# Two routed linear-attention blocks on one core: one load queue, mixed narrow matmuls, scalar_tensor_tensor for small operations, residuals on the TensorE, row-tiled broadcasts

## The chip, the cores and the metric

The kernel runs on one core of one Trainium2 chip. The metric is the device time of one execution in microseconds (us). PE is the TensorE's matmul stream, PEld its weight loads, DVE the VectorE, ACT the ScalarE, POOL the GpSimd, SP the SyncE. "Granted clock" is the TensorE clock that the throttle granted, 1.00 being full speed. In the clock records of before it is 1.00 or 0.50 and nothing else; values between are means over a stretch.

An execution is called slow when it takes over 1.5% more than the fastest of the same kernel in the same set of runs.

## The reference

2048 tokens of 512 channels go through a linear-attention block A and a block B that sends one token through a gated feed-forward, and then through both again with the same weights. "Block one" and "block two" below are the first and the second A+B pair.

```
def A(x, wqkv, wo):                       # 32 heads of 16
    q, k, v = split(x @ wqkv)
    phi = lambda t: where(t > 0, t + 1, exp(t)) + 1e-6
    kv, z = sum over tokens of phi(k) v^T, and of phi(k)      # per head
    o = (phi(q) @ kv) / (phi(q) . z + 1e-6)
    return o @ wo

def B(x, w_r, w_gate, w_up, w_down):
    r = x @ w_r;  i = argmax(r)           # one token of 2048
    y = (silu(x[i] @ w_gate) * (x[i] @ w_up)) @ w_down * sigmoid(r[i])
    return x with y added to row i

x = A_x
x = x + A(layernorm(x));  x = x + B(layernorm(x))
x = x + A(layernorm(x));  x = x + B(layernorm(x))
```

## The kernel before

The kernel is a list of 1120 operations. Each has an engine, the buffers it reads and writes, and one of six general PSUM banks where it needs one; a literal list gives the order and the bank of each buffer. The program is replayed in that order, with semaphores derived from the data. So a change of order or of a bank is a change of that list, and every engine runs its own operations strictly in the listed order.

The parts that the argument touches:

```
# loads: two queues
ldx("sp", 0, 1); ldw("act", "wk", D)            # token tile 0; wk from the ScalarE's queue
ldx("sp", 1, 2); ldw("sp", "wv", 2 * D); ldx("sp", 2, 4) ...

# division by the denominator: the reciprocals (rden, 32 rows per group m) are spread over
# the 128 channels by a matmul with a 0/1 matrix, then multiplied into phi(q)
for m in range(NC_D):                           # NC_D = 4
    bb = bank()
    A("pe",  e.matmul(B(bb), sel[:, m, :], rden[:, j, :]))      # 128 rows, 512 columns
    A("dve", e.tensor_tensor(pqT[:, m, cols], pqT[:, m, cols], B(bb), ALU.mult))

# output tile t of block L
A("pe", four matmuls pqT x Mw into bank ob)
if L == 1 and t in (14, 15):                    # residual by an identity matmul into the bank
    ...
else:                                           # residual on VectorE
    A("dve", e.scalar_tensor_tensor(out=x_tok[:, t, :], in0=x_tok[:, t, :], scalar=scal,
                                    in1=B(ob), op0=mult, op1=add, accum_out=s1[L][:, t:t + 1]))
    A("act", e.activation(junk, x_tok[:, t, :], ACTF.Square, accum_out=s2[L][:, t:t + 1]))

# small statistics on VectorE (128 x 1 to 128 x 16), for instance
e.tensor_scalar(m_, s1[L][:, sl], 1.0 / D, None, op0=mult)
e.tensor_tensor(stat[0][:, 0, sl], rs[1][:, sl], ic[:, sl], mult)

# the final scaling x * us + b of tiles 0 to 10 is on GpSimd, of 11 to 15 on ScalarE
```

The routed feed-forward of the one token is 14 groups of eight matmuls with one column each (L906), and 56 more for the down projection.

Of the kernel before, what the change touches and what calls it, by code (L numbers as in the profile page):

```python
# [24 lines left out]
2 14 26 5 11 12 15 13 10 0 24 34 55 23 6 16 1 21 35 53 25 22 4 17 20 19 46 18 3 52 47 29 33 30 8 31 32 50 9 73  # L25
54 7 57 56 74 58 49 71 59 60 51 72 61 75 83 76 62 48 63 77 80 78 84 85 149 79 96 163 150 86 94 87 81 151 97 88
153 95 164 89 64 90 82 152 167 154 92 91 65 98 174 66 99 165 67 168 100 68 155 93 101 166 175 69 170 70 103
107 102 156 171 27 129 160 108 116 157 104 172 118 181 158 161 173 28 177 182 159 188 140 178 119 141 117 191
105 179 120 189 138 121 195 192 180 162 193 122 36 196 169 176 123 198 194 106 37 125 139 124 109 127 202 142
110 199 111 130 128 38 114 183 143 131 281 126 203 144 39 40 147 132 184 133 41 112 115 223 42 185 145 43 219  # L30
148 224 186 44 45 226 200 187 220 113 134 201 230 227 221 216 146 136 222 190 217 258 228 137 231 229 205 135
197 206 212 207 254 329 213 208 330 251 214 325 255 326 215 209 256 328 327 240 210 204 241 211 218 252 247
242 257 259 243 237 248 282 233 249 238 283 250 277 234 284 225 235 289 236 297 290 278 232 291 309 279 292
261 280 273 310 262 311 285 274 263 312 265 286 275 264 244 287 276 266 288 239 267 245 269 268 246 270 253
260 298 321 271 331 333 332 334 299 305 322 272 335 323 300 306 345 324 336 301 307 346 308 339 302 341 337
340 343 347 317 303 344 338 342 348 304 352 354 318 349 350 313 319 355 293 353 314 351 416 315 294 320 359
417 295 316 418 356 296 360 421 425 423 422 469 361 365 424 470 426 419 471 362 357 420 358 474 476 478 475
368 436 479 433 370 477 371 372 366 430 373 374 363 367 472 427 375 473 364 369 376 522 393 431 392 383 377
483 378 523 386 428 379 432 480 434 381 380 524 437 489 429 394 385 484 435 529 382 525 490 531 395 486 438
526 396 439 599 532 397 491 441 530 595 442 398 443 487 600 527 444 399 606 459 596 481 400 445 528 597 388  # L40
401 602 607 402 446 598 405 447 407 533 448 458 603 410 440 461 408 449 403 384 406 409 482 411 387 601 460
462 534 542 488 452 493 404 535 539 450 543 492 485 389 536 604 540 451 544 456 605 620 541 537 454 569 453
616 571 621 390 494 391 570 546 572 609 495 573 457 496 574 586 585 512 497 513 617 463 623 498 610 618 455
499 630 624 619 611 575 634 500 625 538 576 612 631 626 613 577 501 632 578 584 502 635 464 579 608 587 588
503 412 633 637 614 545 511 505 504 547 615 514 515 548 644 638 580 549 550 562 561 648 506 645 639 551 465
646 640 622 649 627 581 509 552 647 553 554 466 560 413 555 628 507 516 467 641 415 414 510 468 563 564 558
517 629 642 662 556 508 636 663 582 643 651 557 589 672 652 590 559 655 673 653 650 674 654 656 693 583 675
787 694 518 695 565 566 665 568 567 519 683 666 520 521 667 686 684 668 755 687 763 688 756 689 690 757 764
758 657 765 691 799 696 788 766 679 789 676 790 680 591 681 592 677 767 593 594 707 682 708 669 768 711 709
713 727 710 769 715 700 728 712 716 670 714 721 770 729 717 701 722 718 723 800 724 702 719 725 658 801 726  # L50
812 806 810 804 842 805 720 843 802 807 659 775 730 731 808 739 776 732 660 740 733 741 777 661 734 742 735
778 743 736 664 737 703 671 738 809 746 678 811 747 744 685 748 745 749 759 750 751 760 752 753 761 754 762
783 803 814 819 795 813 815 816 784 817 818 785 796 692 820 704 846 821 786 797 771 823 822 798 705 824 779
825 772 826 697 773 780 827 774 828 781 698 782 829 830 831 835 699 836 791 833 837 832 706 838 792 834 839
859 865 793 864 863 866 851 860 794 867 861 852 855 840 868 853 862 925 856 854 871 926 875 857 877 872 869
927 873 858 881 870 878 876 930 874 928 934 882 879 929 847 935 883 969 848 931 890 888 970 891 849 886 884
932 887 971 841 885 844 974 889 972 845 978 975 904 880 973 895 899 903 905 907 896 979 906 900 913 933 897
892 901 898 944 893 902 948 850 908 894 909 914 945 1013 976 910 949 1014 940 977 911 1015 936 941 912 950 980
915 917 937 946 916 1022 918 952 953 942 981 1018 921 1016 988 938 1019 922 1017 1020 982 984 920 924 954 1021
955 956 919 992 1023 985 1024 923 989 986 1028 993 990 961 1037 1025 996 994 1029 1026 1032 960 997 962 1030  # L60
1038 965 1042 1043 998 1027 1040 1039 1044 1031 1033 964 983 987 991 999 995 1045 939 1047 943 1000 1034 947
1001 963 1046 951 1048 1056 1004 1036 1002 1041 1051 1035 957 1003 1005 1058 958 1006 966 1057 1059 967 959
1010 1049 1060 1062 1061 1067 1063 1052 1068 1069 1065 1007 1050 968 1070 1071 1072 1073 1086 1064 1009 1074
1075 1080 1076 1087 1081 1066 1053 1008 1077 1082 1083 1012 1088 1078 1054 1011 1084 1079 1085 1055 1090 1114
1089 1091 1115 1092 1099 1094 1095 1096 1093 1101 1097 1102 1103 1100 1098 1104 1106 1107 1105 1108 1109 1110
1111 1112 1113 1116 1117 1118 1119
"""
BANKS = "303121405672141533202544041250322442535534223501015014433142145253206703250251515044105234030302200131345423544131055442341231215412510530451452232042310010052134345231205420132415041105443453024103350410501554523412023315540231"
# [176 lines left out]
def bass_interleave_layers__linear_attn_block__moe_arch_mod__prompt_kernel(  # L245
# [13 lines left out]
    with ExitStack() as es:  # L259
# [63 lines left out]
        usx = SB("usx", [P, NT], F32)  # L323
        nmr = SB("nmr", [P, NT], F32)
# [90 lines left out]
        ldx("sp", 0, 1)  # L415
        ldw("act", "wk", D)
        A("act", lambda e: e.preload_act_table_set("natural_log_exp_and_others"), writes=["table"], est=1300,
          name="table")
        ldx("sp", 1, 2)
        ldw("sp", "wv", 2 * D)  # L420
        ldx("sp", 2, 4)
# [28 lines left out]
        C("pool", lambda e: e.memset(stat[0][:, 3, :], 1.0), ["stat3"], est=100)  # L450
        C("pool", iota(iota_s[:], [[512, NC_D], [1, P]], -16), ["iota_s"], est=600, name="ios")
        DMA("pool", wr_col[:], B_w_r.rearrange("(c p) -> p c", p=P), ["wr_col"], 4096, "ldwr", after=[ldx3])
        DMA("pool", wr_bc[:], B_w_r.rearrange("(o d) -> o d", o=1).to_broadcast([P, D]), ["wr_bc"], TB, "ldwrb",
# [55 lines left out]

        kv_ctr = [0, 0]  # L510
# [6 lines left out]
        BT = (14, 15)  # L517
# [42 lines left out]
        def kv_out(L, kba, kbb):  # L560
# [35 lines left out]
            if L == 1:  # L596
                rb = bank()

                def rmm(e):
                    ins = None  # L600
                    for m in range(NC_D):
                        ins = e.matmul(B(rb)[:, 2 * m:2 * m + 2], kvT[:, m, :], wow_hl[:, m, :], start=True,
                                       stop=True)
                    return ins
                A("pe", rmm, reads=["kvT", "wow_h", "wow_l"], writes=[rb], est=116, name="mr")
                A("dve", lambda e: e.tensor_reduce(mr_f[:], B(rb)[:, 0:8].rearrange("p (m k) -> p m k", k=2), AX.X,
                                                   ALU.add), reads=[rb], writes=["mr_f"], est=170, name="mrf")
                A("dve", lambda e: e.tensor_copy(mr_hl[:, :, 0], mr_f[:]), reads=["mr_f"], writes=["mr_h"], est=155,
                  name="mrh")
                A("dve", lambda e: e.tensor_tensor(mr_hl[:, :, 1], mr_f[:], mr_hl[:, :, 0], ALU.subtract),  # L610
                  reads=["mr_f", "mr_h"], writes=["mr_l"], est=155, name="mrl")
# [20 lines left out]

        def small(fn, reads, writes, name, est=155, eng="dve"):
            return A(eng, fn, reads=reads, writes=writes, est=est, name=name)
# [19 lines left out]
        def xn_tile(t, mean_ap, scale, nbias, reads, eng, tag):  # L654
# [4 lines left out]
            else:  # L659
                A("pool", lambda e: e.tensor_scalar(xn_tok[:, t, :], x_tok[:, t, :], scale[:, t:t + 1],  # L660
                                                    nbias[:, t:t + 1], op0=ALU.mult, op1=ALU.add),
                  reads=[f"x{t}"] + reads, writes=[f"xn{t}"], est=840, name=f"{tag}xn{t}")
# [26 lines left out]
        dctr = [0]  # L689

        def den_group(L, tg):
# [5 lines left out]
            def den(e):  # L697
# [5 lines left out]
            A("pe", den, reads=[f"pq{tg}_{m}" for m in range(NC_D)] + ["Za", "Zb"], writes=[db], est=500,  # L703
# [4 lines left out]
              reads=[f"lden{j}"], writes=[f"rden{j}"], est=629, name=f"A{L}rden{tg}")  # L708
            for m in range(NC_D):
                bb = bank()  # L710
# [479 lines left out]
        for tg in range(4):  # L1190
# [3 lines left out]
            for g in FG:  # L1194
                if g[0] // 4 == tg:
                    final_group(g, ["pool" if t < 11 else "act" for t in g])
# [58 lines left out]
```

## Time and profile before

Three runs gave 179.29 us (179.17 to 180.23). The profiled execution took 180.61 us, spans 178.8 us, and had a mean clock of 0.932.

| what (profile of before) | value |
|---|---|
| PE busy / VectorE busy | 163.9 / 132.8 us |
| first kv projection starts | 9.66 us |
| last output matmul of block one ends | 81.32 us |
| last router matmul of block one | 108.17 us |
| routed feed-forward starts | 114.61 us |
| row projections of the patched token start | 130.54 us |
| last output matmul of block two ends | 162.36 us |
| last matmul of all starts (routed row, block two) | 175.67 us |

From the profile page: busy times, and the span cut into 40 slices of 4.5 us. Each digit is the busy share of a slice in tenths; PEclk is the granted clock in tenths.

```profile
PE 163.9 (92%) x1393; PEld 84.2 (47%) x1393; DVE 132.8 (74%) x415; ACT 112.3 (63%) x293; POOL 77.4 (43%) x127
...
PE   6599997999999999999999999999999989986393
...
DVE  5699999445589999997961368742466999999830
...
PEclk9999999999999999999999999955799999999555
```

PE is nearly full from slice 7 on (counted from 0), VectorE is full in three stretches (about 9 to 31 us, where PE is full too, 54 to 80 us, and 139 to 165 us), and the clock is halved in slices 26 to 28 and in the last three. The chain of waits that ended last says the same:

```profile
PE 63%; DVE 29%; DMA 3%; POOL 1%; issue 1%; ACT 1%; SPq 0%; POOLq 0%
```

The windows view puts numbers on stages. Its columns are the stretch in us, its length, the busy time and number of instructions of PE, PEld, DVE, ACT and POOL in this order, the granted clock, the DMA share and GB/s.

```profile
57.00:73.00 16.00, 15.89 (x81) 6.54 (x81) 16.00 (x43) 12.15 (x35) 3.37 (x5) 1.00 0.04 9
...
113.00:117.00 4.00, 4.00 (x114) 3.29 (x112) 2.84 (x14) 1.20 (x2) 1.29 (x3) 1.00 0.02 4
117.00:121.00 4.00, 4.00 (x51) 2.96 (x47) 1.26 (x4) 0.61 (x3) 0.00 (x0) 0.51 0.01 4
121.00:124.00 3.00, 3.00 (x61) 2.10 (x60) 1.30 (x6) 0.90 (x3) 0.61 (x1) 0.50 0.00 0
...
145.00:162.70 17.70, 16.96 (x103) 7.51 (x104) 17.70 (x55) 11.78 (x38) 4.47 (x6) 1.00 0.08 31
```

In the first and the last of these lines VectorE is busy for the whole stretch. From 113 to 117 us PE runs 114 matmuls, most of them narrow, at full clock; right after it the clock is 0.5. The records give 10.24 us at half clock from 117.1 us on. The timeline of PE and VectorE (start, us, engine, line, operation, shape, count) shows what this costs, and a small operation that stalls:

```profile
64.74 0.81 PE L711 MATMUL ps<-rden,sel 128*128 128x512 bf16 x3
...
67.99 0.38 PE L711 MATMUL ps<-rden,sel 128*128 128x512 bf16 x1
68.20 1.03 PE L728 MATMUL ps<-Mw,pqT 128*128 128x512 bf16 x4
...
78.02 0.16 DVE L808 TENSOR_SCALAR stat<-rs 128x2 f32<-128x2 f32 x1
78.10 0.59 DVE L799 SCALAR_TENSOR_TENSOR nms<-mv,cs 128x4 f32<-128x4 f32 x1
...
119.40 1.87 PE L620 MATMUL ps<-xnT,wqkv 128*128 128x512 bf16 x4
```

The four 512-wide matmuls at 119.40 span 1.87 us, against 1.02 to 1.04 us for four at full clock elsewhere in this trace. The broadcasts are spread: three in a row, or one alone between output matmuls. The operation at 78.10 writes 128x4 elements and takes 0.59 us; its neighbour at 78.02 (128x2) takes 0.16, and so does one of the same size and form at 78.90 (not shown).

### The profile page before, as it was taken

The page shows a single profiled execution, that of the slowest core. Times are in us where ns is not written, and L with a number is a line of the kernel's source. Part 1 is how long each engine was busy: PE and PEld are TensorE (multiplying, and loading weights), DVE is VectorE, ACT ScalarE, POOL GpSimd, SP SyncE. Part 2 cuts the span into 40 slices and gives each one's busy share as a digit, 9 for nine tenths or more (in the row PEclk, how much of TensorE's full clock was granted, in tenths as well). Part 3 has the DMA queues.
Part 4 walks back from the last instruction along what each step waited for, and adds up shares of the span by engine and source line. Part 5 has one row for each costly group of instructions (what it writes and reads, how often), then busy time and mean ns, then how long its engine had stood idle before and what let it go on. Part 6 is the DMA issues. An engine that isn't in the chain of part 4 may idle for free.

```text
span 178.8 us, 3791 instructions
## 1 busy us (share of the span) xinstructions
PE 163.9 (92%) x1393; PEld 84.2 (47%) x1393; DVE 132.8 (74%) x415; ACT 112.3 (63%) x293; POOL 77.4 (43%) x127
## 2 busy tenths in 40 slices
PE   6599997999999999999999999999999989986393
PEld 2244552554454344454555545685544334434382
DVE  5699999445589999997961368742466999999830
ACT  2287754566569569979975467313456936868920
POOL 5049499544654303084899253501225220336500
PEclk9999999999999999999999999955799999999555
DMA  5995425389960000215144200000000000030450
GB/s 144 396 371 115 64 59 105 72 272 369 377 222 0 0 4 0 59 32 113 37 90 91 59 0 0 4 0 4 0 0 5 0 0 0 0 121 5 168 183 4
DMA packets 23257, 15.83 MB, mean 89 GB/s; under 512 B 15656, under 2 KB 21800, under 8 KB 23112
## 3 DMA queue, kind: packets, MB, share of 16 engines
q1 hardware_dynamic: 22632, 14.95, 28.3%
q10 hardware_dynamic: 528, 0.52, 0.9%
q0 software_dynamic: 80, 0.13, 0.6%
q8 instruction: 11, 0.18, 0.4%
q14 instruction: 6, 0.05, 0.1%
HBM read 9.83 MB, written 2.10 MB: 67 GB/s over the span
## 4 chain that ended last, share of the span: by engine, by line
PE 63%; DVE 29%; DMA 3%; POOL 1%; issue 1%; ACT 1%; SPq 0%; POOLq 0%
PE ps L537 27%; PE ps L620 13%; PE ps L728 8%; DVE pqT L713 6%; DVE x_tok L744 5%; PE ps L554 4%; PE ps L906 3%; DMA x_tok<-in_A_x_dram 3%; DVE scr L480 2%; DVE pqT L506 2%; PE ps L932 2%; PE ps L711 1%; DVE st L667 1%; DVE Mw L594 1%; DVE pk L506 1%
## 5 line engine op out<-in xcount | busy, mean ns | idle before, releaser
L504 POOL TENSOR_SCALAR Eb<-Eb 128x512 bf16<-128x512 bf16 x64 | 39.4, 621 | 59.3 <-ACT Eb L502 50.0
L537 PE MATMUL ps<-wqkv,xnT 128*128 128x512 bf16 x256 | 60.3, 380 | 1.4 <-DVE pk L506 1.3
L502 ACT ACTIVATE Eb<-ps 128x512 bf16<-128x512 f32 x64 | 37.5, 596 | 24.8 <-PE ps L620 12.4
L537 PEld LDWEIGHTS ps<-wqkv,xnT 128*128 128x128 bf16 x256 | 23.7, 98 | 27.7 <-DVE pk L506 1.8
L620 PE MATMUL ps<-xnT,wqkv 128*128 128x512 bf16 x128 | 33.6, 402 | 0.1
L506 DVE SCALAR_TENSOR_TENSOR pk<-ps,Eb 128x512 bf16<-128x512 f32 x32 | 21.6, 686 | 14.4 <-POOL Eb L504 12.0
L728 PE MATMUL ps<-Mw,pqT 128*128 128x512 bf16 x128 | 30.4, 379 | 0.8 <-DVE pqT L713 0.6
L506 DVE SCALAR_TENSOR_TENSOR pqT<-ps,Eb 128x512 bf16<-128x512 f32 x32 | 21.4, 686 | 7.7 <-POOL Eb L504 6.6
L544 ACT ACTIVATE va<-ps 128x512 bf16<-128x512 f32 x32 | 18.7, 596 | 9.2 <-PE ps L537 8.9
L750 ACT ACTIVATE junk<-x_tok 128x512 bf16<-128x512 bf16 x30 | 18.6, 621 | 7.8 <-DVE x_tok L744 7.7
L713 DVE TENSOR_TENSOR pqT<-pqT,ps 128x512 bf16<-128x512 bf16 x32 | 20.3, 680 | 0.0
L728 PEld LDWEIGHTS ps<-Mw,pqT 128*128 128x128 bf16 x128 | 11.8, 98 | 15.8 <-DVE pqT L713 2.5
L620 PEld LDWEIGHTS ps<-xnT,wqkv 128*128 128x128 bf16 x128 | 12.1, 101 | 13.6 <-issue 2.4
L660 POOL TENSOR_SCALAR xn_tok<-x_tok,cs,nms 128x512 bf16<-128x512 bf16 x16 | 12.2, 773 | 9.7 <-DVE stat L813 9.1
L1112 POOL TENSOR_SCALAR xn_tok<-x_tok,us,stat 128x512 bf16<-128x512 bf16 x11 | 8.3, 772 | 13.6 <-DVE mv L777 9.0
L554 PE MATMUL ps<-va,pk 128*128 128x129 bf16 x128 | 12.4, 231 | 0.0
L667 DVE BATCH_NORM_STATS2 st<-x_tok 128x6 f32<-128x512 bf16 x16 | 10.4, 674 | 2.2 <-DMA x_tok<-in_A_x_dram 2.2
L554 PEld LDWEIGHTS ps<-va,pk 128*128 128x128 bf16 x128 | 9.6, 104 | 3.8 <-ACT va L544 0.2
L660 POOL TENSOR_SCALAR xn_tok<-x_tok,rs,nms 128x512 bf16<-128x512 bf16 x12 | 10.9, 915 | 0.4 <-DVE mv L669 0.2
L744 DVE SCALAR_TENSOR_TENSOR x_tok<-x_tok,ps 128x512 bf16<-128x512 bf16 x16 | 10.5, 680 | 0.0
L630 ACT ACTIVATE lnv<-mv,eps_col 128x2 f32<-128x2 f32 (+2 forms) x20 | 5.4, 289 | 8.1 <-DVE mv L669 5.6
L744 DVE SCALAR_TENSOR_TENSOR x_tok<-x_tok,stat,ps 128x512 bf16<-128x512 bf16 x14 | 10.0, 735 | 0.0
(204 smaller groups left out, 194.6 us busy)
## 6 DMA issues: line engine op xcount, KB each, us to landing
out_dram<-xn_tok SPq DMA_DIRECT2D x8, 256.0 KB, 2.1
wu<-in_B_w_up_dram SPq DMA_DIRECT2D x2, 896.0 KB, 8.6
wd<-in_B_w_down_dram SPq DMA_DIRECT2D x2, 896.0 KB, 10.5
wg<-in_B_w_gate_dram SPq DMA_DIRECT2D x2, 896.0 KB, 11.8
wqkv<-in_A_wqkv_dram SPq DMA_DIRECT2D x2, 512.0 KB, 8.7
x_tok<-in_A_x_dram SPq DMA_DIRECT2D x1, 1024.0 KB, 8.7
wqkv<-in_A_wqkv_dram ACTq DMA_DIRECT2D x1, 512.0 KB, 5.3
x_tok<-in_A_x_dram SPq DMA_DIRECT2D x1, 512.0 KB
```

The lines of the kernel that those rows point to most:

```text
L502: A("act", lambda e: e.activation(Eb[:, i, :], src(), ACTF.Exp), reads=[b, "table"], writes=[f"E{i}"], est=600, name=name + "E")
L504: A("pool", lambda e: e.tensor_scalar(Eb[:, i, :], Eb[:, i, :], 1.0, 0.0, op0=ALU.min, op1=ALU.max), reads=[f"E{i}"], writes=[f"E{i}"], es ...
L506: return A("dve", lambda e: e.scalar_tensor_tensor(out=dst, in0=src(), scalar=1e-6, in1=Eb[:, i, :], op0=ALU.max, op1=ALU.add), reads=[b, ...
L537: ins = e.matmul(B(b), xT[:, c, t * P:(t + 1) * P], wqkv[:, c, lo:lo + D], start=(c == 0), stop=(c == NC_D - 1))
L544: A("act", lambda e: e.activation(va[:, i, :].rearrange("p (m k) -> p m k", k=129)[:, :, 0:P], B(vb).rearrange("p (m k) -> p m k", k=P), A ...
L554: ins = e.matmul(views[m], pk[:, i, m * P:(m + 1) * P], va[:, i, m * 129:(m + 1) * 129], start=(first and m in (0, 3)), stop=False, skip_g ...
L620: ins = e.matmul(B(qb), wqkv[:, c, qc * P:(qc + 1) * P], xnT[L][:, c, tg * 512:(tg + 1) * 512], start=(c == 0), stop=(c == NC_D - 1))
L660: A("pool", lambda e: e.tensor_scalar(xn_tok[:, t, :], x_tok[:, t, :], scale[:, t:t + 1], nbias[:, t:t + 1], op0=ALU.mult, op1=ALU.add), r ...
L713: A("dve", (lambda e, m=m, bb=bb: e.tensor_tensor(pqT[:, m, cols], pqT[:, m, cols], B(bb), ALU.mult)), reads=[bb, f"pq{tg}_{m}"], writes=[ ...
L728: ins = e.matmul(B(ob), pqT[:, m, t * P:(t + 1) * P], Mw[:, m, :], start=(m == 0), stop=(m == NC_D - 1 and not xb))
L744: A("dve", lambda e: e.scalar_tensor_tensor(out=x_tok[:, t, :], in0=x_tok[:, t, :], scalar=scal, in1=B(ob), op0=ALU.mult, op1=ALU.add, acc ...
L750: A("act", lambda e: e.activation(junk[:, j, :], x_tok[:, t, :], ACTF.Square, accum_out=s2[L][:, t:t + 1]), reads=[f"x{t}", "table"], writ ...
```

## The change

Its intent: take work off the engine that binds in each stage, and keep PE's clock up.

1. Loads on one queue in the order of need: tiles 0 and 1 in one transfer, then tiles 2 and 3, and wk later.
2. The order is rebuilt so that the feed-forward's narrow groups lie between 512-wide groups.
3. Small VectorE operations become scalar_tensor_tensor (STT).
4. In block two the residuals of tiles 3, 7, 11 and 13 go to PE (identity matmul), with GpSimd preparing those tiles in block one and ScalarE evicting; the final scalings are redistributed (GpSimd 6, ScalarE 5, VectorE 5).
5. The broadcasts become one operation of four 32-row matmuls, each with its own 32 of the 128 rows.

The diff, cut to its core. The order and bank lists are replaced as a whole; most small operations change as the ones shown do.

```
-        ldx("sp", 0, 1)
-        ldw("act", "wk", D)
...
-        ldx("sp", 1, 2)
-        ldw("sp", "wv", 2 * D)
+        ldx("sp", 0, 2)
+        ldw("sp", "wk", D)
+        ldx("sp", 2, 4)
+        ldw("sp", "wv", 2 * D)
...
+        def tt(dst, a, c, op, ...):            # was tensor_tensor
+            return stt(dst, a, 1.0, ALU.mult, c, op, ...)
+        def ts_op(dst, a, s, op, ...):         # was tensor_scalar; one() is a broadcast column of ones
+            return stt(dst, a, s, op, one(shape or dst.shape), ALU.mult, ...)
...
-        BT = (14, 15)
+        XBN = (14, 15)
+        XBA = (3, 7, 11, 13)
+        XB = XBA + XBN
...
+            bbs = [bank() for _ in range(NC_D)]
+                def bcast(e):
+                    for m in range(NC_D):
+                        r = slice(32 * m, 32 * m + 32)
+                        ins = e.matmul(B(bbs[m]), sel[r, m, :], rden[r, j, :], start=True, stop=True)
-            for m in range(NC_D):
-                bb = bank()
-                A("pe", (... e.matmul(B(bb), sel[:, m, :], rden[:, j, :], start=True, stop=True)), ...)
...
+            elif xb:                            # tiles 3, 7, 11, 13 of block two
+                A("act", e.activation(x_tok[:, t, :], B(ob), ACTF.Identity, accum_out=s1[L][:, t:t + 1]))
+                A("act", e.activation(junk[:, j, :], B(ob), ACTF.Square, accum_out=s2[L][:, t:t + 1]))
...
+            for t in xx_:                       # the tiles of XB, in block one
+                A("pool", e.tensor_scalar(x_tok[:, t, :], x_tok[:, t, :], usx[:, t:t + 1],
+                                          nmrx[:, t:t + 1], op0=mult, op1=add))          # "Mx2"
...
-                    final_group(g, ["pool" if t < 11 else "act" for t in g])
+                    final_group(g, ["pool" if t < 6 else ("act", "dve")[t % 2] for t in g])
```

## The prediction

> **What bounds the kernel now.** The instruction profile spans 178.8 us. The chain of waits is 63% PE and 29% VectorE. The windows view gives the stages: from 10 to 137 us PE has no idle worth naming (9.5 to 10.0 us busy in nearly every 10); from 137 to 162.7 us VectorE binds (25.4 of 25.7 us busy); from 162.7 us on there is only the latency chain of the last routed row.
>
> **The clock.** Granted clock is 1.00 except from about 117.1 to 127.3 us and from about 165 us: 0.50. The slow stretch of 10.24 us follows the routed feed-forward: eight-matmul narrow groups run back to back from 114.6 us. Inside it a group of four 512-wide matmuls takes 1.73 us instead of 0.86. It holds 12 to 14 such matmuls (2.7 us lost) and about 20 of 129 columns (1 us lost, estimate): about 3.7 us, nearly all on the chain. [...] In the new order no run of narrow matmuls exceeds the four gathers (1.75 us); the 24 feed-forward pieces are split by 512-wide groups. I think the clock stays full there (75%). The end stays at half clock: no wide work is left.
>
> **Row tiling.** 32 broadcasts of 0.216 us become eight sets of four with 32 rows each. The denominator, four column tiles, occupies about 0.35 us a set (151.14 to 151.47 us); by analogy a set falls from 0.86 to about 0.4 us, 3.5 us of PE in all. Half is in block two, where VectorE binds, and is worth nothing there; in block one VectorE is also full (16.0 of 16.0 us from 57 to 73). I count 1 us.
>
> **Residuals on PE.** Four VectorE residuals (0.68+0.08 us each, 3 us) leave the VectorE-bound stage; PE gains 4 x 0.22 us, ScalarE a reading pass of about 0.8 us per tile (18.9 of 25.7 us busy: room), GpSimd 4 x 0.77 us earlier. Against it, VectorE gets five final scalings of 0.4 us, mostly in the tail. Net 2 us.
>
> **Small VectorE ops as scalar_tensor_tensor.** I expect almost nothing from the conversion itself. Stalled small ops (0.45 to 0.60 instead of 0.15 us) occur beside GpSimd's 512-wide work, but scalar_tensor_tensor with two SBUF inputs stalls already: 0.59 us at 78.10, 0.54 at 156.72. [...] The tail loses about 2 us to such stalls, and they shrink because GpSimd keeps 6 instead of 11 final scalings; VectorE's own scalings take back about half. Net 1 us.
>
> **Loads.** Tiles 0 and 1 in one first transfer, wk no longer beside them: tile 0 landed near 6.4 us, should land near 4; first projection 9.66 us, now about 8.7. Net 1 us, as PE is saturated after it.
>
> Sum: 2.8 (expected clock) + 1 + 2 + 1 + 1, less about 0.3 for copies of statistics and GpSimd's added work from 80 to 100 us (already 67 to 86% busy) = 7.5.
>
> **Prediction: 171.8 us, 80% range 168.0 to 176.0. Faster by over 2%: 0.87; within 2%: 0.11; slower: 0.02.**
>
> **What would show it.** Clock row full until the last stage; broadcast sets near 0.4 us; first projection before 9 us; VectorE-bound stage 2 us shorter; scalar_tensor_tensor small ops still showing 0.4 to 0.6 us stalls beside GpSimd.
>
> **What would make it wrong.** A clock drop in the gathers [...]; four banks held per broadcast set delaying PE; GpSimd late with block two's normalised tiles; a gain in PE absorbed by VectorE.

The sum is 2.8 + 1 + 2 + 1 + 1 − 0.3 = 7.5 us, off before's 179.3. The 2.8 us for the clock is three quarters of the 3.7 us estimated from the trace of before; the 75% was my own estimate.

## The result

The kernel after took 174.69 us (median of 4 runs, 174.48 to 174.85) against 179.76 us for before on the same chip (4 runs, 179.17 to 180.37). The ratio of the times is 0.972, with a 95% interval of 0.968 to 0.976: faster by more than 2%. Ratios here and below are the mean time of one kernel's fast runs over that of the other's fast runs of the same rounds, so they are not quite the ratio of the medians I quote. The time of the profiled execution is not in the later sets' ratios.

The profile after spans 172.9 us at a mean clock of 0.971. It is of a run at full clock, while the profile of before is of one of its slowest (0.932), so the two profiles lie 5.9 us apart where the medians lie 5.1. The same lines as before, page first:

```profile
PE 157.7 (91%) x1397; PEld 80.3 (46%) x1397; DVE 131.3 (76%) x420; ACT 113.4 (66%) x301; POOL 74.6 (43%) x125
...
PE   7999999699998988999999999999999799996492
...
DVE  6965999946387999999864456953675899999931
...
PEclk9999999999999999999999999999999999999855
```

PE's busy time fell by 6.2 us, VectorE's by only 1.5. The clock row has no drop before the end stage. In the chain, PE gave way to VectorE:

```profile
PE 47%; DVE 44%; ACT 4%; POOL 2%; issue 2%; POOLq 0%
```

Windows of after:

```profile
57.00:73.00 16.00, 14.54 (x78) 5.74 (x76) 16.00 (x43) 12.24 (x42) 3.55 (x6) 1.00 0.06 12
...
80.00:90.00 10.00, 9.57 (x54) 4.13 (x52) 7.77 (x32) 8.02 (x28) 9.26 (x14) 1.00 0.44 89
...
113.00:117.00 4.00, 4.00 (x68) 2.57 (x65) 1.58 (x3) 1.28 (x3) 1.29 (x3) 1.00 0.00 0
117.00:121.00 4.00, 4.00 (x62) 2.58 (x60) 1.29 (x5) 2.30 (x7) 1.23 (x2) 1.00 0.00 0
```

In the first line VectorE is again busy for 16.00 of 16 us, while PE has dropped from 15.89 to 14.54: the broadcasts are cheaper, but PE now stands idle for 1.46 us. Of that, 1.03 us lies before one set of broadcasts (65.39 us, below); the trace names a ScalarE operation that ended at 65.37 us, and VectorE's multiplication of the set before ended at 65.33, so the wait cannot be put down to one of them. From 80 to 90 us GpSimd is busy for 9.26 us (6.71 in before). The timeline shows the broadcasts and some stalled small operations:

```profile
65.39 0.39 PE L734 MATMUL ps<-rden,sel 32*128 32x512 bf16 x4 [1.03 <-ACT lden L724]
65.72 3.63 PE L758 MATMUL ps<-Mw,pqT 128*128 128x512 bf16 x16
...
79.69 0.77 POOL L678 TENSOR_SCALAR xn_tok<-x_tok,cs,nms 128x512 bf16<-128x512 bf16 x1 [2.23 <-DVE x2w L521]
...
79.80 0.16 DVE L521 SCALAR_TENSOR_TENSOR stat<-rs,ic 128x4 f32<-128x4 f32 x1
79.88 0.59 DVE L521 SCALAR_TENSOR_TENSOR stat<-rs,ones_mat 128x2 f32<-128x2 f32 x1
...
159.45 0.64 DVE L521 SCALAR_TENSOR_TENSOR stat<-stat,nmr 128x4 f32<-128x4 f32 x1
```

Four broadcasts take 0.33 us from the first to the next matmul (65.39 to 65.72), where four full-height ones took 0.86. The stalls are there as before, now in STT. The small operation at 79.88 begins while GpSimd's scaling of 79.69 runs and ends with it, at 80.47; the one at 79.80 began beside the same scaling and was not held. This is the pattern of both traces: of the 42 stalled small operations of before and after (over 0.26 us; counts under e2), 40 end within 0.03 us of the end of the GpSimd operation beside which they began. They are not slow; they wait it out.

Where did the time go, along the kernel? The table gives the moment at which each kernel's PE had issued the same amount of matmul work. It is my own sum over the trace: each matmul at its full-clock time, leaving out the broadcasts, the identity residuals and the warm-up, which differ. The weight given to narrow matmuls matters: another choice moves single rows by up to 0.5 us.

| before, us | after, us | after minus before |
|---|---|---|
| 8.5 | 7.5 | −1.1 |
| 47.0 | 45.7 | −1.3 |
| 68.0 | 67.9 | −0.1 |
| 81.3 | 80.4 | −0.8 |
| 93.4 | 93.6 | +0.2 |
| 111.5 | 111.9 | +0.4 |
| 128.3 | 124.2 | −4.1 |
| 145.3 | 139.6 | −5.6 |
| 159.7 | 154.1 | −5.7 |
| 171.7 | 165.7 | −6.0 |

So at 111 us, two thirds through, the new kernel is no further than the old one. Its head start from the loads is used up in block one. About 4.5 us come in the routed feed-forward, where before ran at half clock, and some 1.9 after it.

### The profile page after: what moved, and what is told of

The parts are those of the page before. It is cut to its first block, busy times and chain, and to the rows that moved or that the text cites. A ratio compares the mean times of both kernels' runs of the same rounds, so it can differ in the third digit from the quotient of the medians.

```text
span 172.9 us, 3813 instructions
## 1 busy us (share of the span) xinstructions
PE 157.7 (91%) x1397; PEld 80.3 (46%) x1397; DVE 131.3 (76%) x420; ACT 113.4 (66%) x301; POOL 74.6 (43%) x125
## 4 chain that ended last, share of the span: by engine, by line
PE 47%; DVE 44%; ACT 4%; POOL 2%; issue 2%; POOLq 0%
PE ps L560 16%; PE ps L641 11%; DVE pqT L743 11%; DVE x_tok L780 8%; DVE pk L506 5%; PE ps L493 4%; PE ps L938 3%; PE ps L577 3%; DVE st L685 3%; DVE pqT L506 3%; DVE scr L480 2%; PE ps L899 2%; PE ps L758 2%; PE ps L964 2%; DVE stat L521 2%
## 5 line engine op out<-in xcount | busy, mean ns | idle before, releaser
L641 PE MATMUL ps<-xnT,wqkv 128*128 128x512 bf16 x128 | 31.0, 379 | 0.8 <-DVE pqT L743 0.8
L678 POOL TENSOR_SCALAR xn_tok<-x_tok,cs,nms 128x512 bf16<-128x512 bf16 x16 | 12.2, 774 | 14.6 <-DVE nms L834 11.9
L786 ACT ACTIVATE junk<-x_tok 128x512 bf16<-128x512 bf16 x26 | 16.2, 622 | 3.2 <-DVE x_tok L780 2.8
L641 PEld LDWEIGHTS ps<-xnT,wqkv 128*128 128x128 bf16 x128 | 11.6, 98 | 12.6 <-DVE pqT L743 1.1
L678 POOL TENSOR_SCALAR xn_tok<-x_tok,rs,nms 128x512 bf16<-128x512 bf16 x12 | 10.2, 857 | 9.8 <-DVE mv L687 7.9
L1131 POOL TENSOR_SCALAR xn_tok<-x_tok,us,stat 128x512 bf16<-128x512 bf16 x6 | 4.7, 796 | 17.7 <-DVE stat L1119 17.7
L577 PE MATMUL ps<-va,pk 128*128 128x129 bf16 x128 | 11.4, 221 | 0.3 <-DVE pk L506 0.3
L577 PEld LDWEIGHTS ps<-va,pk 128*128 128x128 bf16 x128 | 8.9, 98 | 5.9 <-issue 0.9
L493 PE MATMUL ps<-zeros 128*128 128x512 bf16 x18 | 6.4, 537 | 1.2 <-DVE sign L436 1.2
```

The lines of the kernel that those rows point to most:

```text
L577: ins = e.matmul(views[m], pk[:, i, m * P:(m + 1) * P], va[:, i, m * 129:(m + 1) * 129], start=(first and m in (0, 3)), stop=False, skip_g ...
L641: ins = e.matmul(B(qb), wqkv[:, c, qc * P:(qc + 1) * P], xnT[L][:, c, tg * 512:(tg + 1) * 512], start=(c == 0), stop=(c == NC_D - 1))
L678: A("pool", lambda e: e.tensor_scalar(xn_tok[:, t, :], x_tok[:, t, :], scale[:, t:t + 1], nbias[:, t:t + 1], op0=ALU.mult, op1=ALU.add), r ...
L786: A("act", lambda e: e.activation(junk[:, j, :], x_tok[:, t, :], ACTF.Square, accum_out=s2[L][:, t:t + 1]), reads=[f"x{t}", "table"], writ ...
```

## The experiments

All kernels gave correct results. Each ran with its profile and then five rounds (e9 and e11: six) beside the kernel before, in four sets on three chips. The record calls each of these comparisons with before "unclear"; before's own runs spread, as told next. What each part is worth is therefore read from marks. Marks are read from the profiles; within one order they repeat to about 0.02 us once the start (which jitters by up to 0.5 us) is taken off. One run of before at 236 us, far from all others, is left out of every number here.

One warning for reading the ratios. Before's own runs fall into groups by mean clock: in these four sets, 10 of 45 had a clock of 0.967 or more and took 176.4 to 177.3 us; the 33 with less than 0.96 had a median of 179.4 us. In the result's own four runs of before, none was that short. In later sets some were, and only those and runs up to 1.5% longer are "fast". So later ratios are nearer to 1 for the same kernel, and I compare marks, and run times at equal clock.

### The clock and the mixing of narrow matmuls

**c_after**: the kernel after, unchanged, as a control in a later set.

> The changed kernel itself again, as the control of this job and to see whether its own time is one number. Three of six runs of the form with plain small operations showed a mean granted clock of 0.96 instead of 0.97 and 1.6 us more. Theory [...]: two groups of runs about 1.6 us apart, the slower one with the lower mean clock. Rival (the mixed order never falls): one group near 174.7 us, clock 0.96 to 0.972.

Measured: 176.1 us median; three runs at 174.88 to 175.67 us with a clock of 0.965 to 0.971, and three at 176.52 to 176.66, all at 0.959. Ratio 0.990 (0.980 to 1.001). The profiled run was one of the long ones. Its windows show why:

```profile
137.00:145.00 8.00, 6.60 (x32) 2.05 (x29) 6.23 (x12) 4.89 (x10) 0.99 (x2) 0.79 0.00 0
```

A clock of 0.79 over 8 us is 3.4 us at half clock, in a place where before and after had none; the records say 3.41 us. PE is idle for 1.5 us between 130 and 140 us just before it; in the profile after, the same idle time was followed by no drop. From the first output matmul of block one to that of block two every mark is 0.50 to 0.51 us later than in the profile after (the start), and the last output matmul 1.96 us later. So one such stretch cost 1.45 us, and the new kernel meets it in some runs.

**e5_bunched**: the kernel after, with the narrow groups of the feed-forward put together again in one stretch of about 2.8 us; only the order list changes.

```
 order: B0g0 B0u0 ... B0g6 | every remaining B0g*, B0u* moved to here, back to back
```

> The changed kernel with the 14 groups of narrow matmuls of the routed row's first feed-forward products moved into one bunch of 2.8 us; no work is added. Theory (the mixing matters through the granted clock): the clock falls to 0.5 near 115 us for 3.4 to 10.2 us, and the kernel is 2.0 to 4.5 us slower. Rival (the mixing matters through what waits for what): the clock row stays full and the time within 0.7 us.

Measured: 176.52 us (174.98 to 177.10), ratio 0.988 (0.980 to 0.996). In the profile, the clock fell at once:

```profile
113.00:117.00 4.00, 4.00 (x80) 2.58 (x78) 0.87 (x2) 0.38 (x1) 0.66 (x2) 0.71 0.02 4
117.00:121.00 4.00, 4.00 (x25) 2.04 (x23) 0.99 (x3) 1.98 (x7) 0.61 (x1) 0.86 0.00 0
```

Half clock for 3.41 us, and all marks from the down projection on are 1.63 us later; from the first output matmul up to there they are as in after within 0.02. The direction held; the size is short of the 2.0 us expected. It is close to that of one half-clock stretch in c_after, so little is left for the order itself. The trace shows no PE idle time between 110 us and the drop (114.72 us); the last 2.8 us before it are the narrow groups. One of the six runs (174.98 us, clock 0.965) seems to have escaped it.

**e6_before_mixed**: the kernel before, with only its feed-forward order changed (and two buffers' banks exchanged for it): pieces of one or two narrow groups between 512-wide ones.

```
-order: ... B0u0 B0g0 B0u2 B0g2 B0u4 B0g4 B0u6 B0g6 B0u8 B0g8 ... (ten in a row)
+order: ... B0u0 A1q1_1E B0g0 ... A1kv9 A1q0_1 B0u4 B0g4 ... A1kv10 A1q1_3 ... B0u8 B0g8 ...
```

> The kernel before, with only the order around the routed row's feed-forward changed: its narrow groups are cut into four pieces by 512-wide groups that were due later. Theory (the granted clock is what the mixing buys): the clock row is full until the last stage and the span is 3 to 4.5 us below the 178.8 us of the profile of before, which had 10.24 us at half clock; against the mean of the fast runs of before, whose mean clock differs from run to run, 1.5 to 3.5 us. Rival (order alone): within 0.7 us.

Measured: 178.19 us (177.92 to 178.55), ratio 1.004 (0.995 to 1.013). The profile has full clock until the end stage and ends 2.6 us before that of before. But its runs, at clocks of 0.957 to 0.967, take 178.2, and the two runs of before on the same chip that escaped the drop take 176.6. So in the old order mixing removes the halved clock (the profile shows it, and the six runs lie within 0.63 us) and costs about 1.6 us of its own: it makes the time steadier, at 1.1 us under before's median of 179.3, and not faster than before at its best.

**What follows for the clock.** 176.6 us against 174.7 to 174.9 us is before and after both without a drop (before's from other sets than the result's). So of the 5.1 us between the medians of the result, about 1.8 us is work and order, and 3.2 us (179.76 less 176.6) is the clock.

### The broadcasts

**e1_bc_full**: the kernel after, with four full-height broadcasts in place of the 32-row ones, in the same place.

```
-                        ins = e.matmul(B(bbs[m]), sel[r, m, :], rden[r, j, :], start=True, stop=True)
+                        ins = e.matmul(B(bbs[m]), sel[:, m, :], rden[:, j, :], start=True, stop=True)
```

> The changed kernel with the broadcast's four matmuls put back to the full 128 rows (same order, same banks): a set should take 0.86 us of PE again instead of 0.33, 4.3 us of PE over eight sets. Theory (VectorE paces both output stages, so PE time there is not on the chain): 0.3 to 1.2 us slower than the changed kernel. Rival (PE time counts in full, as PE was the engine of most of the chain before): 3.5 to 4.3 us slower.

Measured: 177.43 us (176.90 to 177.91), ratio 0.995 (0.988 to 1.001). The start is 0.35 us late; the last output matmul of block one is 2.02 us late, of block two 3.12, the end 2.76. Row tiling is worth about 2.4 us in the new order: 1.7 gained in block one's output stage (0.4 given back by the routing), 1.1 more in block two. Both expectations missed: it is more than I had allowed, and less than the PE time saved. That saving is itself smaller than 0.86 less 0.33 suggests, because the step from a full-height matmul into a 32-row set takes 0.31 us where it takes 0.22 into a full-height one: from the matmul before a set to the one after it, where nothing waits, it is 0.64 us in after and 1.08 here. (From the first of four to the next full-height matmul, 0.86 against 0.33 us is 2.6 times; with the longer step into the set counted, 0.86 against 0.42 us, 2.0 times.) Over the eight sets, waits included, the sums are 8.19 and 11.75 us, 3.6 us apart. From 57 to 73 us VectorE waits 2.0 us for these broadcasts in e1, and not at all in after.

**e7_before_rowtile**: the kernel before with 32-row broadcasts, nothing else.

```
-            e.matmul(B(bb), sel[:, m, :], rden[:, j, :], start=True, stop=True)
+            e.matmul(B(bb), sel[32 * m:32 * m + 32, m, :], rden[32 * m:32 * m + 32, j, :], start=True, stop=True)
```

> The kernel before with each broadcast matmul reading only the 32 rows it needs, so that neighbours in the queue can overlap; order and banks untouched. In that order the four of a set are often apart. Undone in the changed kernel this part cost 2.75 us. Theory (overlap needs neighbours): gain of 0.5 to 2 us here. Rival (the size alone counts): 2.5 us or more.

Measured: 179.98 us (176.78 to 180.66), ratio 1.006 (0.987 to 1.025); the end mark differs from before's by +0.04 us. Nothing, where the theory had 0.5 to 2. The timeline of PE in e7 shows the reason, at the place quoted from before above:

```profile
64.69 0.44 PE L711 MATMUL ps<-rden,sel 32*128 32x512 bf16 x3
...
68.04 0.39 PE L711 MATMUL ps<-rden,sel 32*128 32x512 bf16 x1
68.36 1.04 PE L729 MATMUL ps<-Mw,pqT 128*128 128x512 bf16 x4
```

In the old order the broadcasts are not four in a row. Five of the 32 stand alone. From a lone 32-row broadcast to the next full-height matmul it is 0.32 us, from a lone full-height one 0.22 us, and the step into it takes 0.31 us against 0.22: each costs 0.2 us more. Only neighbours overlap (0.003 to 0.004 us from one to the next): at the three places where three stand in a row and nothing waits, the stretch from the matmul before to the one after falls to 0.63 us from 0.86 to 0.96. In the other sets later members start 0.06 to 0.6 us apart. Over all 32, waits included, these stretches sum to 11.34 us in before and 11.57 in e7, so PE saved nothing. The gain of row tiling comes from tiling and reordering together; neither the tiling in the old order nor, as e1 shows, the new order without the tiling has it.

### Residuals and small operations

**e3_res_dve**: the kernel after with the residuals of tiles 3, 7, 11, 13 back on VectorE (and GpSimd's and ScalarE's work for them gone).

```
-        XBA = (3, 7, 11, 13)
+        XBA = ()
```

> The changed kernel with the residuals of tiles 3, 7, 11 and 13 of block two back on VectorE; GpSimd's four scalings for them and eight small copies of statistics are gone too. Theory: the stage that VectorE bounds (about 137 to 157 us) gets up to 3 us longer, the stretch from 77 to 93 us, where GpSimd works 86 to 93% of the time, up to 1 us shorter; in sum 1.0 to 2.5 us slower than the changed kernel. Rival (what VectorE saves is eaten by the added scalings): within 0.5 us.

Measured: 175.98 us (175.87 to 179.65, one slow), ratio 0.988 (0.980 to 0.997). Marks against after: the same to the last output matmul of block one; from the last router matmul of block one (102 us) to the first output matmul of block two 0.93 us earlier; the last output matmul 0.26 us later; the end 1.31 us later. So moving these residuals saves 2.2 us at the end and costs 0.93 us in block one: net 1.3. Of the 2.2 us, 1.2 come up to the last output matmul and 1.06 between it and the gather (5.07 us in after, 6.13 here, 6.15 in before): VectorE's last residual ends at 158.10 us here, 0.36 us after the last output matmul, and at 156.39 in after, 1.09 us before it.

**e10_mx2_late**: the kernel after, with that preparation moved. GpSimd's six scalings "Mx2" start at 86.8 to 97.2 us in after, between the normalisations that the transposed tiles of block two wait for; here they start at 100.1 to 115.3 us. Eight copies of statistics on VectorE move too. Order only.

> The changed kernel with GpSimd's six scalings for the residuals on PE, and eight small copies of statistics on VectorE, moved from the stretch of 77 to 93 us, where GpSimd is busy 86 to 93% of the time, to the stretch from 95 to 115 us, where it is half idle. Theory (this is what the residuals on PE cost, 0.93 us at 100 us in the run that took them off): 0.6 to 1.2 us faster than the changed kernel at equal clock. Rival (the loss is only moved): within 0.3 us.

Measured: 174.43 us (173.81 to 175.05), ratio 0.983 (0.973 to 0.993), on the chip where c_after had 176.1. Against c_after, whose profile starts 0.1 us later, the last router matmul comes 1.06 us sooner and the row projections 0.70. At equal clock (0.971) the runs are 174.22 against 174.88 us, one run each. This fits e3: the 0.93 us are mostly the place of this preparation, and 0.6 to 0.7 us of them can be had back by order alone.

**e2_plain_small**: the kernel after, with all converted small operations as tensor_tensor and tensor_scalar again.

```
-            return stt(dst, a, 1.0, ALU.mult, c, op, reads, writes, name, est)
+            return small(lambda e: e.tensor_tensor(dst, f(a), f(c), op), reads, writes, name, est)
-            return stt(dst, a, s, op, one(shape or dst.shape), ALU.mult, ...)
+            return small(lambda e: e.tensor_scalar(dst, f(a), s, None, op0=op), ...)
```

> The changed kernel with its two helpers for small VectorE operations issuing tensor_tensor and tensor_scalar again instead of scalar_tensor_tensor, nothing else. Theory [...]: within 0.5 us of the changed kernel, and 0.4 to 0.6 us stalls of small operations in like number (17 in the changed kernel's trace). Rival (the form matters): 1.5 us or more slower, with clearly more stalls.

Measured: 175.92 us (174.44 to 176.48), ratio 0.986 (0.977 to 0.994); three runs with a clock of 0.967 to 0.971 at 174.44 to 175.37, and three at 176.5 with 0.959 to 0.960, like c_after's run with a drop. All marks are 0.10 to 0.21 us later, and the first projection is 0.21 us late already. The conversion by itself is worth nothing that can be seen. The count of stalls agrees: of the small operations (STT, tensor_tensor, tensor_scalar, cast; up to 64 elements a partition) that began beside a 512-element GpSimd operation, 20 of 60 took over 0.26 us in after and 19 of 60 in e2 (22 of 67 in before). Of the 108 that began with none running, none did in after. Two inputs are not a condition: five of the 22 in before (two casts and three tensor_scalar, one of them 0.60 us at 165.81) read a single tensor.

### The loads

**e4_two_queues**: the kernel after, with wk on the ScalarE's queue from the start and tiles 0 and 1 as two transfers.

```
-        ldx("sp", 0, 2)
-        ldw("sp", "wk", D)
+        ldx("sp", 0, 1)
+        ldw("act", "wk", D)
+        ldx("sp", 1, 2)
```

> The kernel after with the start of its loads undone: wk from a second queue (ScalarE) at the start, token tiles 0 and 1 as two transfers of 128 KB. Theory (the load gain of about 1 us is real and stays): the first transposes come 0.7 to 1.2 us later, and the end of the profile too, 0.7 to 1.3 us later than after's 172.9. Rival (the gain is given back in block one's output stage, where VectorE paces both kernels): the start is late by as much, but the difference is under 0.4 us from the last output matmul of block one on, and the end moves by under 0.4 us.

Measured: 176.1 us (175.94 to 177.45), ratio 0.994 (0.988 to 1.000). The first transposes are 1.34 us later than in after, and so is everything else, to the end: +1.46 at block one's output stage, +1.40 at the last matmul. Tiles 0 and 1 landed at 3.69 us in after; here tile 0 landed at 3.54 and tile 1 at 5.59 (before: 4.36 and 6.43). The theory held: a microsecond at the start is a microsecond at the end. The head start that the table of equal work shows vanishing in block one was not absorbed by a stage that VectorE paces; it was spent on other things there. The 0.93 us of e3 are one part of that.

### Two orders of the tail, and a faster version

**e8_tail**: the kernel after, with VectorE's order changed from 157 us on: two statistics that stall beside GpSimd (0.67 and 0.64 us) and the final scalings come after the routing maximum.

> The kernel after with VectorE's order changed in the last stage only: the statistics and the final scalings of tiles 8 to 15 (two of them stall to 0.67 us beside GpSimd) come after the routing maximum, the scalings after the gather has been released. Theory (order on VectorE, not any engine's total, sets the time from the last output matmul to the gather: 5.08 us in after's profile): all marks up to the last output matmul as in after within 0.1 us, the maximum 0.7 to 1.3 us sooner, the gather 0.8 to 1.5 us sooner, the end 0.8 to 1.5 us sooner. Rival (ScalarE's chain of moments and the row's eviction set it): under 0.4 us.

Measured: 174.94 us (174.73 to 175.46), ratio 0.986 (0.981 to 0.991). The profile began 0.91 us late; taking that off, the gather comes 0.57 us sooner and the end 0.19 us sooner. The theory missed its range. VectorE's timeline shows where it went:

```profile
159.69 0.62 DVE L521 SCALAR_TENSOR_TENSOR rt<-rt,x2w 128x2 f32<-128x2 f32 x2
160.34 0.79 DVE L521 SCALAR_TENSOR_TENSOR r_bf<-rt,stat 128x4 bf16<-128x4 f32 x3
```

The operations that now stand beside GpSimd's last scalings (156.3 to 161.0 us) stall in place of the ones moved away: 0.62 us for two and 0.79 for three, where after took 0.22 and 0.29. Another 0.38 us is lost between the gather and the end (7.53 us, in after 7.14): two final scalings on VectorE (0.73 us from 164.26) now stand ahead of the sum that the routed row needs, which starts 2.02 us after the gather instead of 1.55.

**e9_combo**: e10 and e8 together, and one thing more. Four reductions on VectorE for the router of block two (L480, up to 1.14 us each with GpSimd beside them) run at 28 to 32 us in after, where PE waits 1.5 us for VectorE; they move to VectorE's idle time at 111 to 117 us. Order only.

> A version meant to beat both: the late GpSimd order of e10, the tail order of e8_tail, and the four router-weight reductions on VectorE (scr, about 1.1 us each at 28 to 32 us, where PE waits 1.7 us) moved to VectorE's idle time in the routed feed-forward. If the parts add: PE's wait near 32 us is gone, the last r of block one 1.0 us or more sooner than in after, end of the profile 170.2 to 171.7 us, time ratio to before 0.955 to 0.972. If the 28 to 32 us wait was only slack that block one's output stage takes back, its part is 0 and the profile ends 171.3 to 172.0.

Measured: 172.63 us (172.23 to 173.75, 7 runs), ratio 0.972 (0.967 to 0.977), in a set where before had 179.16. At clocks of 0.964 to 0.971 it takes 172.2 to 172.8 us. That beats after by about 2.1 us and before by 6.5 us in the medians, and before at its best (176.4) by 3.8. PE's wait near 32 us is gone (PE is not idle from 20 to 40 us, against 1.5 us in after). The mark at the end of block one's projections is 1.67 us sooner than in after, and it stays 1.67 sooner to the end of block one's output stage. So this wait was not slack either. The last router matmul is 2.59 us sooner. The profiled run, the slowest of the seven, met a half-clock stretch like c_after's (0.79 over the same window), so its end is only 1.0 us ahead.

**e11_pool_early**: e9_combo, with the scale and bias of tiles 0 to 7 written as soon as their moments are known, so that GpSimd's final scalings start earlier; tile 7 goes to GpSimd, and the tail's statistics fill VectorE's waits for PE.

> e9_combo with GpSimd's final scalings started some 5 us sooner (VectorE writes the scale and bias of tiles 0 to 7 as soon as their moments are there, not after the residuals), tile 7 given to GpSimd, and the statistics of the tail spread into VectorE's waits for PE. Theory (the slow small operations are those beside GpSimd's wide ones, whatever their instruction, and in e8_tail they only moved to other small operations: two at 0.61 us and three at 0.79 us together just ahead of the maximum): GpSimd is done before 157 us, no VectorE operation of 64 elements or fewer from 156 us to the end takes over 0.3 us, the time from the last output matmul to the gather falls from e9_combo's 4.5 us to 3.0 to 3.8 us, and the end comes 0.8 to 1.8 us sooner for an equal start and clock: 170.6 to 172.0 us. Rival (the stalls are not GpSimd's doing, or something else sets the tail): the stalls stay, and the end moves by under 0.4 us.

Measured: 172.93 us (172.33 to 176.08), ratio 0.978 (0.974 to 0.982). GpSimd's stretches moved as meant, and the small operations behind them are fast:

```profile
151.75 3.02 POOL L1131 TENSOR_SCALAR xn_tok<-x_tok,us,stat 128x512 bf16<-128x512 bf16 x4 [12.89 <-DVE stat L521]
155.35 2.27 POOL L1131 TENSOR_SCALAR xn_tok<-x_tok,us,stat 128x512 bf16<-128x512 bf16 x3 [0.58 <-DVE stat L521]
```

```profile
157.04 0.59 DVE L521 SCALAR_TENSOR_TENSOR mv<-s,ones_mat 128x4 f32<-128x4 f32 x1
...
160.53 0.28 DVE L521 SCALAR_TENSOR_TENSOR rt<-rt,x2w 128x2 f32<-128x2 f32 x2
160.85 0.16 DVE L521 SCALAR_TENSOR_TENSOR r_bf<-rt,stat 128x4 bf16<-128x4 f32 x1
161.25 0.30 DVE L521 SCALAR_TENSOR_TENSOR r_bf<-rt,stat 128x2 bf16<-128x2 f32 x2 [0.24 <-ACT stat L651]
```

The two and the three that took 0.62 and 0.79 us now take 0.28 and 0.46. The last stall of over 0.3 us, at 157.04, is also the last small operation that starts beside GpSimd (which ends at 157.62). So it is GpSimd that makes them slow: that part of the theory held. The gain in time did not come. At a clock of 0.969 the runs are 172.65 and 172.69 us, and e9's 172.61 and 172.81. From the last output matmul to the gather it is 4.8 us, against 4.5 in e9. In place of the stalls VectorE now waits for the ScalarE (the bracket above: 0.24 us, and 0.19 us at 159.51), whose moments of the last tiles became the next link. On that the rival was right.

Its profiled run, at 176.08 us, is worth a look for the clock. Here a drop reaches into the mixed feed-forward, but begins before it:

```profile
110.00:113.00 3.00, 3.00 (x54) 1.90 (x53) 2.50 (x12) 0.68 (x2) 1.41 (x3) 0.50 0.02 5
113.00:117.00 4.00, 4.00 (x27) 1.74 (x26) 2.38 (x6) 0.60 (x1) 1.36 (x2) 0.57 0.00 0
```

The half clock begins at 109.63 us and lasts 6.83 us. The first feed-forward matmul starts only at 111.20; just before the drop are the gathers, 64 one-column matmuls in a row from 106.81 to 108.5 us, which this order does not mix. So this looks like the risk that the prediction named (a clock drop in the gathers), met in one of the eleven profiles of the new order and its variants; no run isolates it. Why the clock stayed low for 6.83 us, into the mixed part, is open.

## Why the prediction was right or wrong

"Faster by over 2%" and the range (168.0 to 176.0) held. The point, 171.8 us, was 2.9 us too low. Term by term, in the order of the prediction:

| term | predicted | measured | from |
|---|---|---|---|
| clock | 2.8 | 2.7 to 3.2 | before's median (179.3, and 179.76 in the result's runs) less its runs without a drop (176.6), e5, e6 |
| row tiling | 1 | 2.4 undone in after, 0 done in before | e1, e7 |
| residuals on PE | 2 | 1.3 (2.2 saved, 0.93 paid) | e3 |
| small operations: conversion | about 0 | about 0 | e2 |
| tail | 1 | 1.1 (last output matmul to last matmul: 13.3 to 12.2 us), but part of the residuals' 2.2 | profiles, e3 |
| loads | 1 | 1.3 to 1.4 | e4 |
| copies and GpSimd's added work | −0.3 | −0.93, inside the residuals' line | e3, e10 |
| sum | 7.5 | 5.1 | result |

**Right.** The first projection came at 8.66 us, a broadcast set takes 0.33 us, the clock row was full to the last stage, stalls of 0.4 to 0.67 us stayed in STT operations. "PE is saturated after it", and therefore the whole load gain counts, is shown by e4. (The tile was misread: tile 0 landed at 4.36 us in before; it was tile 1 that landed at 6.43.) That the conversion to STT buys nothing is shown by e2. An STT of after with a column of ones as its second input took 0.59 us at 79.88 and ended with GpSimd's operation. Beside a 512-element GpSimd operation such small operations took up to 0.67 us; with none running, no small operation of after took over 0.24. e11 shows it the other way round.

**Wrong: "Half is in block two, where VectorE binds, and is worth nothing there".** Undoing the tiling cost another 1.1 us in block two, and 1.7 us in block one's output stage, where I had argued with the same full VectorE. VectorE busy for 16.00 of 16 us does not mean that PE's time is free. The broadcast is a link between two VectorE operations: the sooner it ends, the sooner VectorE has its operand. In e1 VectorE is busy for only 15.54 us of the same window and waits for the broadcasts. But the opposite rule would be no better: done alone in before, it gave nothing, because there PE's own time did not fall (11.34 and 11.57 us, e7).

**Wrong in size: "Net 2 us" for the residuals, and "less about 0.3".** The 2.2 us saved are of the size predicted, but only 1.2 of them lie in the stage that VectorE binds; 1.06 come after it, before the gather. The price was three times what I put down, because GpSimd was put to work on the tiles of block two just when it also had to deliver the normalised tiles that PE waits for (moved out of the way, 0.6 to 0.7 us came back: e10). The prediction named this risk ("GpSimd late with block two's normalised tiles") and gave it no weight.

**Wrong: "VectorE-bound stage 2 us shorter".** From the first to the last output matmul of block two it is 17.4 us in before and 18.2 us in after. It would have been 19.3 us without the residuals on PE (e3). The stage starts with other work in the new order, so its length by itself was no measure of the residuals.

**Unproven: the tail's own "Net 1 us".** It was to come from fewer stalls, as GpSimd keeps 6 instead of 11 final scalings. The 1.1 us are there, but e3 has the same split of scalings and its tail takes 13.27 us, as long as before's 13.31. So the gain goes with the residuals, and the term was counted twice.

**Wrong: the sum.** Without the clock, the terms predicted 4.7 us and before and after at their best differ by 1.8 us. Yet undone one by one in the new order, tiling (2.4), loads (1.4) and residuals with the tail (1.3) come to about 5.1 us. So the shortfall is in none of these parts. One item on the other side is measured: mixing cost about 1.6 us in the old order when the clock was full in both (e6). The prediction had counted what mixing saves and not what it costs; that it costs as much in the new order was not measured. The rest, about 1.7 us, was not settled. That the new order was built around these parts, and pays for each with waits elsewhere, is the likely reading, because e7 shows a part worth 2.4 us in one order and nothing in the other; but it is an argument, not a measurement.

**The clock was right for the average, and partly luck.** By their times (179.17 us or more) all four runs of before in the result had a drop, and all four of after escaped it (174.48 to 174.85). The prediction took the one profile of before for every run. With 10 of 45 runs of before at 176.4 to 177.3 us and three of six runs of c_after at 176.5 to 176.7, the same two kernels can also be compared at nearly 1.00. Half-clock stretches ahead of the end stage lasted 3.41 us (c_after, e5), 6.83 us (e11) and 10.24 us (before), and the same order meets one in some runs and none in others. What decides when the clock falls is not settled by these runs. In before and e5 it fell where PE had not been idle (4.00 busy us from 113 to 117 us in before, with 114 matmuls, most of them narrow); in c_after 1.5 us of PE idle time came just before. The profile of e11 fell after the gathers (109.63 us); that of after, with 64 of them in a row too (1.75 us from 108.50 us), did not.

## What to carry to other kernels

Before you explain a gain, sort the runs of both kernels by mean granted clock: here 3.2 of 5.1 us were the clock, and one profile could not tell. A part of a change must be undone in the new order and also done alone in the old one; row tiling gave 2.4 us in the one and nothing in the other, because only adjacent row tiles overlapped (0.003 to 0.004 us from one to the next, e7) and each lone change to 32 rows and back cost 0.2 us. And once the engines' totals fit, look for an engine that is made to wait by work nobody needs yet: moving such work on GpSimd and VectorE to idle stretches, with changes of order alone (e9, the tail's order among them), gave another 2.1 us.
